# Six more constant products among the transposes of the first head

## The chip, the cores and the metric

The kernel runs on one core of one Trainium2 chip. The metric is device time in microseconds (us) of one execution. A profile shows one execution; its span, from the first to the last instruction, is about 1.7 us shorter than the time (304.4 against 306.14 us before). In these traces TensorE multiplies, VectorE and ScalarE copy, cast and apply functions, GpSimd and SyncE issue most transfers (62 and 92 of 157 in the profile before). All runs told here gave the right result, and those whose state could be judged were fast; a run with a single execution has the state "unknown".

## The reference

```python
# attention over 4 x 8 heads, 768 positions of 64 values, with a mask of 32-blocks
scores = scale * np.matmul(q, k.transpose(0, 1, 3, 2))
...
attn = np.exp(scores); attn = attn / attn.sum(-1, keepdims=True)
x = np.matmul(attn, v)            # heads side by side: (4, 768, 512)
# then a residual MLP
tok = np.einsum('ts,bsd->btd', w_tok, alpha1 * x + beta1)
u = x + lam * tok
out = u + lam * (np.maximum((alpha2 * u + beta2) @ w_ch1, 0) @ w_ch2)
```

## The kernel before

Instructions are placed in a fixed order on each engine by a small planner, which runs when the kernel is built. Ahead of the plan stands a hand-written start for the first head. The parts that matter are these.

```python
def keep_warm(n, w, to=gbT[3]):
    for _ in range(n):          # products of constants; nobody reads the result
        nc.tensor.matmul(to[:, 0:w], ones[:, 0:P], ones[:, 0:w], start=True, stop=True)

keep_warm(6, 512)
keep_warm(1, P)
...                             # VectorE makes the block mask
for w in (0, 1):                # mask product, 24 rows
    nc.tensor.matmul(bq_ps[w][0:NBLK, 0:HS], mbb[MB, :], kx2[0][MB, 0, ts(w, HS)], ...)
...                             # casts of q (VectorE) and k (ScalarE, VectorE)
keep_warm(3, P)
for w, bk, o0, o1, cp in (
    (0, gbT[0], 0, 3, nc.vector.tensor_copy),   # q: three transposes
    (1, gbT[1], 0, 1, nc.scalar.copy),          # k: one
    (1, gbT[2], 1, 3, nc.vector.tensor_copy),   # k: two
):
    t = transposes(bk[:], lambda o: relp[:, 0, w, ts(o, P)], range(o0, o1))
    for r in range(2):
        cp(out=qkr[0][:, w, 0, o0:o1, r, :], in_=t[r * D : (r + 1) * D, o0:o1])
keep_warm(3, P)
...                             # from here on the plan: scores, exponentials, ...
```

The plan's first work is the scores of the first head (five products make two "units" of 1024 columns), seven constant products, the scores of the third unit, six transposes for the second head, one constant product, and the scores of the fourth unit. An exponential on ScalarE follows each unit. On VectorE the plan begins with copies of the mask rows and two casts of q and k for the second head.

The softmax here doesn't subtract the row's maximum and nothing guards it: scores larger than these inputs give would overflow.

## Time and profile before

| | before |
|---|---|
| time, median of three | 306.14 us (305.75 to 306.19) |
| span of the profile | 304.4 us |
| TensorE busy | 99% |
| first product of 128 columns with its full-rate duration (219 ns) starts at | 9.70 us |
| first, fourth, fifth exponential start at | 6.96, 10.44, 11.61 us |

One more view is of use for the comparison: the chain that ended last in order of time, from 4.9 to 9.9 us. The columns are start, duration and what the chain passes through.

```profile
4.89 0.31 ACT relp L541
5.19 0.05 issue
5.24 0.50 PE gb L517 x3
5.74 0.32 PE gb L485 x3
6.06 1.72 PE sps L1019 x5
7.78 0.75 PE gb L485 x7
8.53 0.85 PE sps L1019 x3
9.38 0.54 PE gb L517 x6
```

After the cast of k on ScalarE the chain lies on TensorE alone, through products (L1019 scores, L485 constants, L517 transposes) that still run at half rate (314 ns for 128 columns at 5.5 us, 219 ns from 9.70 us on).

### The profile page before, as it was taken

What the parts mean: (1) busy time and instruction counts of PE and PEld (TensorE: products, weight loads), DVE (VectorE), ACT (ScalarE), POOL (GpSimd) and SP (SyncE); (2) the same over time, 40 slices, a digit from 0 to 9 for tenths busy, and PEclk for the clock granted to TensorE, in tenths of its full rate; (3) what the DMA queues carried; (4) which work ended last, traced back from release to release, by engine and by line L of the source; (5) the groups of instructions that cost most, each with busy time, mean ns of one, the idle gap of its engine ahead of it and who ended that gap; (6) DMA issues with size and microseconds to landing.
All of it is one profiled execution on the core that took longest, in us unless ns stands there. A gap on an engine that the chain in (4) does not pass through costs nothing.

```text
span 304.4 us, 7164 instructions
## 1 busy us (share of the span) xinstructions
PE 300.4 (99%) x2991; PEld 187.9 (62%) x2991; DVE 233.5 (77%) x441; ACT 177.4 (58%) x242; POOL 44.6 (15%) x71
## 2 busy tenths in 40 slices
PE   8999999999999999999999999999999999999996
PEld 3777888766656575566655575555664674665443
DVE  7688899988988995989977886668869681997212
ACT  4999998978778755775486756654657720000000
POOL 9447451150110110020000000000000000000000
DMA  7999999998884959074173423050021004000112
GB/s 157 202 255 209 204 205 180 186 201 138 139 132 91 155 114 164 36 113 93 38 119 45 113 49 74 36 145 4 37 52 43 28 2 122 37 0 0 71 65 73
DMA packets 50672, 31.38 MB, mean 103 GB/s; under 512 B 27784, under 2 KB 47056, under 8 KB 50640
## 3 DMA queue, kind: packets, MB, share of 16 engines
q0 software_dynamic: 17520, 15.47, 32.8%
q1 hardware_dynamic: 32796, 15.06, 21.9%
q8 instruction: 23, 0.38, 0.5%
q10 hardware_dynamic: 324, 0.39, 0.4%
q14 instruction: 9, 0.07, 0.1%
HBM read 30.78 MB, written 6.29 MB: 122 GB/s over the span
## 4 chain that ended last, share of the span: by engine, by line
PE 96%; DVE 2%; ACT 1%; issue 0%; ACTq 0%
PE gb L1529 27%; PE gb L1449 27%; PE gb L1081 12%; PE gb L1302 10%; PE sps L1019 8%; PE sps L1038 4%; PE gb L1038 3%; PE gb L517 2%; PE gb L485 2%; DVE qk L578 1%; ACT eT L1057 0%; ACT qk L576 0%; DVE wtokT L578 0%; DVE ot L1551 0%; DVE x_sb L1100 0%
## 5 line engine op out<-in xcount | busy, mean ns | idle before, releaser
L1057 ACT ACTIVATE eT<-sps 128x1024 f16<-128x1024 f32 x114 | 110.8, 1030 | 9.4 <-PE gb L1081 5.7
L1449 PE MATMUL gb<-uT,w1b 128*128 128x384 bf16 (+1 forms) x512 | 91.8, 326 | 0.0
L1529 PE MATMUL gb<-w2b,hts 128*128 128x512 bf16 (+2 forms) x400 | 89.4, 370 | 0.0
L1449 PEld LDWEIGHTS <-w1b 128*128 128x128 bf16 x512 | 48.6, 98 | 33.7 <-issue 1.9
L1062 DVE TENSOR_TENSOR eT<-eT,msk 128x1024 f16<-128x1024 f16 x90 | 59.6, 683 | 6.5 <-ACT eT L1057 6.4
L1529 PEld LDWEIGHTS <-hts 128*128 128x128 bf16 x400 | 36.7, 98 | 38.9 <-issue 1.9
L1057 ACT ACTIVATE eT<-gb 128x512 f16<-128x512 f32 x60 | 32.5, 594 | 33.8 <-PE gb L1038 31.8
L1496 DVE TENSOR_SCALAR hts<-gb,b1t 128x384 bf16<-128x384 f32 x73 | 44.8, 617 | 9.1 <-PE gb L1449 7.6
L1081 PEld LDWEIGHTS <-eT 128*128 128x128 f16 x1152 | 44.3, 97 | 10.8 <-issue 2.2
L1081 PE MATMUL gb<-vext,eT 128*128 128x65 f16 x1152 | 47.9, 193 | 0.1
L1488 ACT ACTIVATE hts<-gb,b1t 128x384 bf16<-128x384 f32 x55 | 31.5, 581 | 21.4 <-PE gb L1449 19.1
L1302 PE MATMUL gb<-a1p,wtokT 128*128 128x256 bf16 (+1 forms) x360 | 37.0, 251 | 0.0
L1551 DVE TENSOR_TENSOR ot<-x_sb,gb 128x512 f32<-128x512 f32 (+2 forms) x25 | 16.6, 664 | 26.0 <-PE gb L1529 26.0
L1302 PEld LDWEIGHTS <-wtokT 128*128 128x128 bf16 x360 | 29.5, 98 | 6.8 <-issue 1.9
L1019 PE MATMUL sps<-qk 88*128 88x512 bf16 (+1 forms) x144 | 32.6, 336 | 0.2
L1326 DVE TENSOR_TENSOR x_sb<-x_sb,gb 128x512 f32<-128x512 f32 (+1 forms) x26 | 16.7, 641 | 2.9 <-PE gb L1302 2.6
L1100 DVE TENSOR_TENSOR x_sb<-gb,rcp 128x384 f32<-128x384 f32 x32 | 17.8, 557 | 1.1
L1038 PE MATMUL sps<-qk 64*128 64x256 bf16 x180 | 17.9, 305 | 0.0
L1038 PEld LDWEIGHTS <-qk 64*128 64x128 bf16 x240 | 9.3, 94 | 11.5 <-issue 7.1
L1097 DVE RECIPROCAL rcp<-gb 128x6 f32<-128x6 f32 x32 | 6.1, 192 | 13.3 <-PE gb L1081 13.2
L1340 DVE TENSOR_TENSOR ub<-x_sb,a_bc 128x512 bf16<-128x512 f32 (+1 forms) x26 | 16.1, 644 | 0.3
L647 POOL DMA_DIRECT2D v<-in_v_dram x15 | 10.6, 703 | 36.6 <-DVE vext L1119 24.9
(70 smaller groups left out, 173.8 us busy)
## 6 DMA issues: line engine op xcount, KB each, us to landing
out_dram<-ot SPq DMA_DIRECT2D x23, 256.0 KB, 2.0
v<-in_v_dram POOLq DMA_DIRECT2D x16, 192.0 KB, 7.9
k<-in_k_dram POOLq DMA_DIRECT2D x15, 192.0 KB, 7.3
q<-in_q_dram POOLq DMA_DIRECT2D x15, 192.0 KB, 7.5
w1b<-in_moe_w_ch_dram POOLq DMA_DIRECT2D x4, 512.0 KB, 11.8
w2b<-in_moe_w_ch_dram POOLq DMA_DIRECT2D x4, 512.0 KB, 16.9
qk<-qk SPq DMA_DIRECT2D x20, 96.0 KB, 2.3
wtk<-in_moe_w_tok_dram POOLq DMA_DIRECT2D x3, 384.0 KB, 8.2
```

Source lines behind the costliest of these rows:

```text
L1019: nc.tensor.matmul(spsT[sl(key[0])][:, o : o + w], kx2[i][0:KC, a, ts(jt, P)], qx2[i][0:KC, a, c : c + w], start=True, stop=True,)
L1038: nc.tensor.matmul(half(key, r)[:, o : o + w], kd[i][rows, h, g, :], qx2[i][rows, h, c : c + w], start=True, stop=True,)
L1057: nc.scalar.activation(out_, in_, AF.Exp, bias=EXPB, scale=SCALE)
L1062: nc.vector.tensor_tensor(out=e, in0=e, in1=msk[:, :, x : x + 512], op=ALU.mult)
L1081: nc.tensor.matmul(bk[:, t * VW : t * VW + D + 1], eTt[sl(("eT", i))][:, ts(col, P)], vx[:, a, jt, 0 : D + 1], start=(r == 0), stop=(r >= ...
L1100: nc.vector.tensor_tensor(out=x_sb[:, s0 : s0 + NT, h * D : (h + 1) * D], in0=o[:, :, 0:D], in1=rc[:].unsqueeze(2).broadcast_to([P, NT, D] ...
L1302: nc.tensor.matmul(bank(bk)[:, j * wp * P : (j + 1) * wp * P], wtokT[:, s, ts(m * g + j, P)], a1p[sl(ak)][:, s, 0:wp, :].rearrange("p w c ...
L1326: nc.vector.tensor_tensor(out=s, in0=s, in1=tp, op=ALU.add)
L1449: nc.tensor.matmul(bank(bk)[:, 0 : HS + w0], w1b[:, dk, ts(f, P)], rhs[dk], start=(dk == 0), stop=(dk == 3),)
L1488: nc.scalar.activation(htsT[hk][:, f, :], bank(bk)[:, w0 : HS + w0], AF.Relu, bias=b1t[:, f : f + 1], scale=1.0,)
L1496: nc.vector.tensor_scalar(out=htsT[hk][:, f, :], in0=bank(bk)[:, w0 : HS + w0], scalar1=b1t[:, f : f + 1], scalar2=0.0, op0=ALU.add, op1=A ...
L1529: nc.tensor.matmul(bank(ck)[:, cs], htsT[hk][:, nk, ts(mt, P)], w2h["t"][:, nk, cs], start=(nk == 0), stop=(nk == 15),)
```

## The change

The intent is to fill the gaps that TensorE still has before the first scores; the author assumed that its rate then doubles earlier. The whole diff is this.

```diff
     keep_warm(6, 512)
-    keep_warm(1, P)
+    keep_warm(2, P)
...
         t = transposes(bk[:], lambda o: relp[:, 0, w, ts(o, P)], range(o0, o1))
+        keep_warm(1 if w else 4, P)
         for r in range(2):
```

One product is added ahead of the mask product, four between the transposes of q and k, and one after each of the two groups of k. The order of everything else stays.

## The prediction

> **What bounds the kernel now.** I began with the page: the slices of busy tenths, then the chain that ended last.
>
> ```profile
> PE   8999999999999999999999999999999999999996
> ACT  4999998978778755775486756654657720000000
> ...
> PE 96%; DVE 2%; ACT 1%; issue 0%; ACTq 0%
> ```
>
> The reader is to see that TensorE is full in all 40 slices (7.6 us each) and holds 96% of the chain, and that ScalarE is as full only in slices 2 to 6. So work added to TensorE costs time wherever it doesn't land in one of its gaps. The change touches only the first 6 us, so I next read the groups by shape of TensorE, once up to 6.2 us, then from 9.7 to 31 us.
>
> ```profile
> L485 PE MATMUL gb<-const-bfloat16-1.0 128*128 128x128 bf16 x7 | 1.3, 310 | 0.0
> L517 PE MATMUL gb<-identb,relp 128*128 128x128 bf16 x6 | 1.0, 310 | 0.1
> L1019 PE MATMUL sps<-qk 88*128 88x512 bf16 x1 | 0.6, 586 | 0.0
> ```
>
> ```profile
> L1019 PE MATMUL sps<-qk 88*128 88x512 bf16 x29 | 9.9, 379 | 0.1
> L517 PE MATMUL gb<-identb,q 128*128 128x128 bf16 x18 | 2.0, 219 | 0.0
> L485 PE MATMUL gb<-const-bfloat16-1.0 128*128 128x128 bf16 x4 | 0.9, 219 | 0.0
> ```
>
> The same product of 128 columns takes 310 ns early and 219 ns late; the distance from one start to the next goes from 107 ns to 56 ns, and for 512 columns from 427 ns to about 216 ns. TensorE streams at half rate at first. The profile's clock column says 1.00 in all these stretches, so it does not show this; only durations do. One by one, the transposes starting at 9.17, 9.28 and 9.39 us take 314 or 315 ns, those at 9.49, 9.60 and 9.70 take 311, 260 and 219 ns. The step between the starts at 9.599 and 9.696 is 97 ns; 128 columns at 1.2 per ns first and 2.4 after give 87 ns of half rate, so the rate doubled at about 9.68 us.
>
> Third, the timeline of ScalarE, which runs the exponentials:
>
> ```profile
> 5.56 0.55 ACT L552 COPY qk<-gb 64x128 bf16<-64x128 bf16 x2 [0.38 <-PE gb L517]
> 6.96 1.94 ACT L1057 ACTIVATE eT<-sps 128x1024 f16<-128x1024 f32 x2 [0.85 <-PE sps L1019]
> 9.42 13.71 ACT L1057 ACTIVATE eT<-sps 128x1024 f16<-128x1024 f32 x14 [0.52 <-PE sps L1019]
> 23.32 7.61 ACT L1057 ACTIVATE eT<-sps 128x1024 f16<-128x1024 f32 x8 [0.19 <-PE sps L1019]
> ```
>
> It waits for scores at 6.96 and at 9.42 us, and then hardly at all up to 31 us. Whatever brings the first scores forward therefore moves a long row of exponentials with it.
>
> Fourth, the waits in the stretch 4.7 to 5.3 us:
>
> ```profile
> PEld L517 <- ACT relp L541: 0.4, 1, 0.4
> ```
>
> This is the largest real gap of TensorE: products stream until 4.894 us, then the first transpose of k starts at 5.240, after ScalarE's cast (ended 5.184).
>
> [...]
>
> **The change part by part.** It adds six constant products of 128 columns and removes nothing. The order of all other instructions on all engines is unchanged when the two builds are compared. At half rate they cost 6 x 107 = 0.64 us of array time.
>
> 1. One more after the first seven. Stream ended 3.400, next product 3.537: 0.107 us fit in a gap of 0.137. Free.
> 2. Four between the transposes of q and of k: 0.427 us in a gap of 0.346. The first transpose of k goes from 5.240 to about 5.322: 0.08 us late.
> 3. One each after the first and after the last transposes of k. There is no gap there: before, the stream ran on from 5.240 to 5.854, and scores start at 5.914. Now three transposes, two new products and the three old ones end at 5.322 + 8 x 0.1065 = 6.175. The first scores are 0.26 us late.
>
> So taken alone the change costs 0.26 us of TensorE, and about 0.31 us at the first exponential, which must wait for the third product. Its only possible reward is the earlier rate change. [...]
>
> What that gives, followed forward with durations of this trace. First product of scores from 6.175: [...] the two of 256 columns at about 109 ns each start at 6.436 and 6.545; the last, 272 ns long, ends at 6.82, so the first exponential starts near 6.85 (before 6.96). The second follows 0.92 us later as in the trace, 7.77 (7.88). Scores of the third unit wait for the end of the first exponential, 7.88, plus 0.05: 7.93, then 109 + 109 + 377 ns end at 8.53; before, the seven products ahead of them held them to 8.319 and they ended at 9.38. Third exponential near 8.75 instead of 9.42. Here a new wait comes up: the transposes of the second head need VectorE's casts, which ended 8.739 and become some 0.1 us later because of step 2. So they begin near 8.93 (before 9.17), six and one constant product take 7 x 0.056 = 0.39, scores of the fourth unit 0.43 plus 0.16 of drain, fourth exponential 9.96 (10.44). Then 24 products with v, 0.73 us, and the scores of the fifth unit, 0.43: 10.49 + 0.43 + 0.17 = 11.1 against 11.57. Net **0.49 us** gained, with the cost of step 3 already inside. [...]
>
> Does it last? From 11.6 to 31 us ScalarE idles 0.34 us in all and TensorE about 1.5 us, nearly all waiting for exponentials, which move along. After 31 us TensorE has almost no gap. Transfers cannot move, their engines being 90% busy or more up to 76 us; but from the landing records, loads land before first use by 1.2 us (q, 10.22 against 11.41), 0.9 (q, 25.97 against 26.89), 0.8 (v, 33.44 against 34.28) and 0.9 to 1.0 (w2 slices, 58.01 against 58.95, 61.14 against 62.16). All exceed 0.5. So 0.49 us should reach the end: 306.14 - 0.49 = 305.65.
>
> **The rivals.** Rival one: the rate still changes at 9.68 us. [...] Then the lateness of step 3 stays: 306.14 + 0.3 = 306.4. Rival two: the change comes even earlier[...]. Scores then start when VectorE is ready, near 5.9, and the first exponential near 6.6; casts again hold the second head, so some 0.8 us in all, 305.3. [...] Rival three: full rate earlier but all of it swallowed by ScalarE or loads: the slacks above speak against it, time 306.1.
>
> **Range and chances.** I give 0.55 to the change[...] (305.65), 0.15 to earlier still (305.3), 0.25 to no change of the rate (306.4), 0.05 to swallowed. The middle lies at about 305.7; with a run noise of some 0.2 us, 305.0 to 306.5. 2% is 6.1 us[...]: within 2%, 0.98.
>
> **What would show it.** In the profile after, transposes of the second head (near 9 us) should have about 219 ns instead of 314, and scores of 512 columns after 6.3 us 379 instead of 634. The first exponential should start near 6.85, the third near 8.75, the fifth near 11.1. If the first starts near 7.27 and the transposes still take 314 ns, rival one holds. If the constant products at 5 us are already at 219 ns, rival two. If the fifth exponential is 0.5 us early and the span isn't, some wait between 11 and 80 us took it, and the slack argument is wrong.

Terms of the sum place the doubling after the change: the first product of the scores, in which the author took it to fall and which ends at 6.436 us. The sum came to a gain of 0.49 us and 306.14 - 0.49 = 305.65 us; without that assumed moment it doesn't follow. The terms also counted the gaps of TensorE: 0.137 + 0.140 + 0.346 + 0.060 = 0.68 us between 3.40 and 5.91 us in the trace of before, and by the author's estimate 0.030 + 0.140 = 0.17 us after the change. That fewer gaps bring the doubling forward was assumed. The 1.2 and 2.4 columns per ns are 512 columns over the measured 427 and about 216 ns.

## The result, and the profile after

The first comparison gave 305.69 us (305.58 to 305.89, six runs) against 306.14 us (305.75 to 306.59, six runs). The ratio is 0.9985, 95% interval 0.9972 to 0.9998. Ratios here are the mean time of one kernel's fast runs over that of the other's of the same rounds, so they are not quite the ratio of the medians. In later rounds of the same two kernels this gain shrank or vanished; that is told with the experiments. All outputs are right.

The slices and the chain by engine of the changed kernel, from its page:

```profile
PE   8999999999999999999999999999999999999996
ACT  4999999978778755775486756554557720000000
...
PE 91%; DVE 6%; ACT 1%; issue 1%; ACTq 0%
```

TensorE is as full as before, but VectorE has grown from 2% to 6% of the chain. The groups by shape up to 6.2 us, with the mean duration after the busy time:

```profile
L485 PE MATMUL gb<-const-bfloat16-1.0 128*128 128x128 bf16 x14 | 1.8, 250 | 0.0
L517 PE MATMUL gb<-identb,relp 128*128 128x128 bf16 x6 | 0.7, 224 | 0.1
L1020 PE MATMUL sps<-qk 88*128 88x512 bf16 x1 | 0.4, 376 | 0.0
```

The transposes take 224 ns instead of 310, the first scores 376 instead of 586. Here the rate doubled before the transposes: the product starting at 4.46 us took 314 ns, those at 4.57, 4.68 and 4.75 took 287, 237 and 219. ScalarE's timeline:

```profile
5.61 0.55 ACT L553 COPY qk<-gb 64x128 bf16<-64x128 bf16 x2 [0.32 <-PE gb L517]
6.61 2.85 ACT L1058 ACTIVATE eT<-sps 128x1024 f16<-128x1024 f32 x3 [0.45 <-PE sps L1020]
9.84 12.68 ACT L1058 ACTIVATE eT<-sps 128x1024 f16<-128x1024 f32 x13 [0.37 <-PE sps L1020]
22.71 7.61 ACT L1058 ACTIVATE eT<-sps 128x1024 f16<-128x1024 f32 x8 [0.19 <-PE sps L1020]
```

The first exponential is 0.36 us earlier (6.61 against 6.96), the third 0.98 us (8.43 against 9.42), but the fourth only 0.61 us (9.84 against 10.44), and the fifth again 0.61 us (11.00 against 11.61). What came up between is seen in the waits of the stretch 7 to 9.3 us:

```profile
PEld L517 <- DVE relp L512: 0.9, 1, 0.9
...
PE gb L517 <- DVE relp L512: 0.5, 1, 0.5
```

and in the chain in order of time:

```profile
7.73 0.35 DVE qk L997
8.08 0.03 issue
8.11 0.64 DVE relp L512 x2
8.75 0.05 issue
8.80 0.51 PE gb L517 x6
```

TensorE now stands until 8.80 us for VectorE's two casts. These ended at 8.741 us after the change and at 8.739 before, so the transposes of the second head gained only 0.37 us (8.80 against 9.17). The chain goes through VectorE where it had gone through TensorE. Of the 0.61 us at the fifth exponential, 0.49 us are left at 34 us (a copy on ScalarE at 33.92 instead of 34.41), and 0.4 us in the span (304.0 against 304.4). The trace shows what took the difference: one copy on VectorE (L1119 before, L1120 after), on which the work behind it waited. Before, then after:

```profile
32.49 0.35 DVE L1119 COPY vext<-v 128x768 f16<-128x768 f16 x1
```

```profile
31.89 0.53 DVE L1120 COPY vext<-v 128x768 f16<-128x768 f16 x1
```

From 41 us on the exponentials of the two profiles stay 0.43 to 0.44 us apart up to the last one at 239 us. Why the same copy took longer here is not known.

### The profile page after: what moved, and what is told of

Its sections match the earlier page's. It is cut to its first block, busy times and chain, and to the rows that moved or that the text cites. A ratio compares the mean times of both kernels' runs of the same rounds, so it can differ in the third digit from the quotient of the medians.

```text
span 304.0 us, 7157 instructions
## 1 busy us (share of the span) xinstructions
PE 297.9 (98%) x2977; PEld 187.1 (62%) x2998; DVE 234.1 (77%) x441; ACT 177.5 (58%) x242; POOL 44.6 (15%) x71
## 4 chain that ended last, share of the span: by engine, by line
PE 91%; DVE 6%; ACT 1%; issue 1%; ACTq 0%
PE gb L1450 27%; PE gb L1530 27%; PE gb L1082 11%; PE gb L1303 9%; PE sps L1020 5%; PE sps L1039 4%; PE gb L1039 3%; PE gb L517 2%; PE gb L485 1%; DVE qk L579 1%; DVE a1p L1265 1%; DVE a1p L1254 1%; ACT eT L1058 0%; ACT qk L577 0%; DVE x_sb L1101 0%
## 5 line engine op out<-in xcount | busy, mean ns | idle before, releaser
L1530 PE MATMUL gb<-w2b,hts 128*128 128x512 bf16 (+2 forms) x379 | 87.2, 370 | 1.1
L1020 PE MATMUL sps<-qk 88*128 88x512 bf16 (+1 forms) x144 | 31.3, 325 | 0.5 <-ACT eT L1058 0.3
L648 POOL DMA_DIRECT2D q<-in_q_dram x15 | 10.7, 710 | 35.3 <-DMA qk<-q 29.7
```

Of the source, the lines that this page charges most:

```text
L1020: nc.tensor.matmul(spsT[sl(key[0])][:, o : o + w], kx2[i][0:KC, a, ts(jt, P)], qx2[i][0:KC, a, c : c + w], start=True, stop=True,)
L1530: nc.tensor.matmul(bank(ck)[:, cs], htsT[hk][:, nk, ts(mt, P)], w2h["t"][:, nk, cs], start=(nk == 0), stop=(nk == 15),)
```

## The experiments

Two theories stood at the start. **The work decides** (theory 2 in the expectations): the moment of the doubling follows from the products issued, and the gap of 0.35 us at 4.9 us delays it in the kernel before. **Free moment** (theory 1): the moment isn't tied to the kernel, so it differs from run to run, and one profile of each kernel is one draw. All twelve runs were used. The table collects the looks; each row is one profiled execution, with its time at the end. "Full rate" is the start of the first product that has its full-rate duration (219 to 230 ns for 128 columns; 256 columns took 270 to 272 ns at full rate and 421 at half rate in before).

| run | what it is | full rate | exponential 1 / 4 / 5 | time of this execution |
|---|---|---|---|---|
| first profile | before | 9.70 | 6.96 / 10.44 / 11.61 | 306.14 |
| b2 | before again | 4.55 | 6.46 / 9.79 / 10.96 | 305.85 |
| b3 | before again | 4.67 | 6.46 / 10.15 / 11.31 | 306.00 |
| b4 | before again | 5.24 | 6.51 / 9.83 / 11.00 | 305.74 |
| first profile | changed | 4.75 | 6.61 / 9.84 / 11.00 | 305.73 |
| a2 | changed again | 6.15 | 6.85 / 10.06 / 11.22 | 305.95 |
| a3 | changed again | 4.07 | 6.25 / 9.83 / 11.00 | 305.75 |
| a4 | changed again | 5.75 | 6.74 / 9.83 / 11.00 | 305.78 |
| p_first | first product only | 4.14 | 6.32 / 9.84 / 11.00 | 305.80 |
| p_gap | changed, without the four | 4.08 | 6.61 / 9.83 / 11.00 | 305.54 |
| p_four | the four only | 4.99 | 6.54 / 9.82 / 10.99 | 305.77 |
| p_four2 | the four only, again | 5.32 | 6.54 / 9.83 / 11.00 | 305.70 |
| no_warm | no constant products ahead | 10.31 (256 columns) | 7.04 / 10.73 / 11.89 | 306.69 |
| cast_first | changed, casts earlier | 5.85 | 6.73 / 9.46 / 11.08 | 306.13 |

### The kernel before, looked at again (b2, b3, b4)

No edit. Expected:

> The kernel before once more, unchanged, for one look at when the rate of TensorE doubles. Theory 1[...]: the doubling need not be at 9.68 us again[...]. Theory 2 (the moment follows from the work alone: the gap of 0.35 us at 4.9 us delays it): 9.7 us again within 0.2 us. Time 306.1 in either case.

> The kernel before a third time, for one look. By now before has doubled at 9.68 and at 4.46 us, the changed kernel at 4.63 and 6.06. [...] First exponential 6.45 to 6.6 if early, 6.96 if late.

> The kernel before a fourth time, for one look; the same as for b3. If the moment is free, b3, b4 and the two earlier looks shall not all agree.

Measured: the unchanged kernel reached full rate at 4.55, 4.67 and by 5.24 us. In b4 there was no product between 4.89 and 5.24 us, and the one at 4.785 already took only 281 ns. b2's groups from 4.5 to 6.2 us and its ScalarE:

```profile
L517 PE MATMUL gb<-identb,relp 128*128 128x128 bf16 x6 | 0.7, 220 | 0.4 <-ACT relp L541 0.4
```

```profile
6.46 2.86 ACT L1057 ACTIVATE eT<-sps 128x1024 f16<-128x1024 f32 x3 [0.41 <-PE sps L1019]
9.79 4.12 ACT L1057 ACTIVATE eT<-sps 128x1024 f16<-128x1024 f32 x4 [0.47 <-PE sps L1019]
```

This is the profile that the change was meant to bring about, with the 0.4 us gap still in it and without the change. The second theory is right on the point that counts: the moment is not fixed by the kernel. (What moves it is not shown.) b3 adds something else. Its fourth exponential is late (10.15) although its rate doubled early, because a small load (be2T) held VectorE for 0.65 us ahead of the same two casts, which ended near 9.05. So the casts paced this stretch, and their delay cost about 0.3 us at the fourth exponential (9.79 in b2, 9.83 in b4) although the rate had doubled.

### The changed kernel again (a2, a3, a4)

No edit. Expected:

> The changed kernel once more, unchanged. Theory 1: the doubling is at another moment than 4.63 us[...], and the time is 305.5 to 306.0. Theory 2: 4.63 us again within 0.2 us. The time over that of before: 0.9985 as in the first comparison, in either case.

> The changed kernel, to see its spread over runs. So far 28 runs of before lie from 305.48 to 306.63, 13 of them above 306.1; 12 of the changed kernel from 305.55 to 306.07. Theory: before doubles late[...], the changed kernel never does, so the change cuts off the slow part of the spread. Then all six runs here lie under 306.2, before again has about a third above 306.2[...]. Rival: both kernels have the same spread and the twelve were luck; then a third of these runs is above 306.2 too.

> The changed kernel again, as a3: all under 306.2 by the theory, about two of six above 306.2 by the rival. The doubling in the look at a moment other than in the earlier ones.

Measured: full rate from 6.15, 4.07 and 5.75 us, again a different moment each time. The late fourth exponential of a2 (10.06) is not the work of its doubling: as in b3, be2T came late (7.71 us, against 6.47 in the first profile of before), and the casts ended at 8.97. Times: a2 305.71 us median (six runs, 305.55 to 306.07), before 305.88 in the same rounds, ratio 0.9993 [0.9980, 1.0007]. a3 305.69 (five runs, 305.53 to 305.76) and a4 305.79 (five runs, 305.53 to 306.58), before 305.55 (nine runs, 304.98 to 306.54), ratios 1.0000 [0.9987, 1.0012] and 1.0008 [0.9993, 1.0024]. The first comparison's 0.15% did not come back. Putting all rounds together (which were not all run at one time nor on one chip, so this is a rougher comparison than one within rounds), 40 times of before (with the three single ones of b2 to b4) have a mean of 305.90 us, 22 of the changed kernel 305.75 us. The difference is 0.15 us, with a 95% interval of plus or minus 0.16 us worked out from the two spreads, so it isn't clear of zero. Above 306.2 us lie 8 of the 40 and 1 of the 22. That would fit a change that trims the slow part of the spread, but a4's 306.58 contradicts "never", and the counts are too small to show it.

### Parts of the change (p_first, p_four, p_gap, p_four2)

p_first is the kernel before with this edit:

```diff
-    keep_warm(1, P)
+    keep_warm(2, P)
```

> Only the first of the added products (the eighth, ahead of the mask product). Its 0.107 us should show as a later start of the 24-row product (3.64 instead of 3.54 us), since the pause of 0.137 us before that product stays as it is. Theory 2 in the form that the stream up to 4.6 us decides: doubling near 4.63 us as in the changed kernel, and its whole gain, 305.7. Theory 1: the gap at 4.9 us is untouched, so the doubling has the same spread as before; 306.1 to 306.3.

p_four, and p_four2 again, are the kernel before with this one:

```diff
         t = transposes(bk[:], lambda o: relp[:, 0, w, ts(o, P)], range(o0, o1))
+        keep_warm(0 if w else 4, P)
```

> Only the four products between the transposes of q and k. They fill the largest gap. Both theories: if it is this gap that keeps the doubling late, this part has the whole gain, or a little more than the whole change because 0.2 us of other products are absent: 305.5 to 305.7[...]. If the gap doesn't matter: 306.1 to 306.4 and a doubling that is late.

> Only the four products, a second time. The first time gave 305.50 to 306.30, two of six above 306.2. Theory that this gap alone decides: five or six of six under 306.2 and a mean of 305.7, as the changed kernel. If two or more of six are again above 306.2, the four alone do not remove the slow part, and the other two parts of the change, or other causes such as the landing of loads, have a share in it.

p_gap is the changed kernel without its four products:

```diff
-        keep_warm(1 if w else 4, P)
+        keep_warm(1 if w else 0, P)
```

> The changed kernel without its four products between the transposes of q and k, so with the gap at 4.9 us open again and the other two parts kept. Theory: the slow part of the spread is back, one to four of six runs above 306.2, mean 305.9 to 306.2. Rival (the first product or the two late ones matter): all under 306.2.

Measured: p_first 305.76 us, ratio 0.9999 [0.9985, 1.0014]; p_four 305.74, ratio 0.9997 [0.9983, 1.0011]; p_gap 306.21, ratio 1.0016 [1.0001, 1.0031]; p_four2 305.76, ratio 1.0008 [0.9992, 1.0024]. Of p_four's eleven times in the two rounds three lie above 306.2, which is more than the expectation allowed. No part shows a gain. p_gap is a little slower than before in its own rounds, with three of five above 306.2; that agrees in direction with the idea that the open gap brings slow runs, but before has the same gap and had only one of nine above 306.2 in those rounds. So these times don't settle which part matters.

The trace of p_first does settle what the first product costs. TensorE's timeline of before, then of p_first, from 3.2 us:

```profile
3.54 0.49 PE L522 MATMUL sps<-qk,mbb 24*24 24x384 bf16 x1
```

```profile
3.64 0.40 PE L522 MATMUL sps<-qk,mbb 24*24 24x384 bf16 x1
```

The 24-row mask product starts 0.10 us later. In both kernels it starts 0.137 us after the stream of the 128-row product ahead of it ended (3.400 to 3.537; 3.505 to 3.642 in the changed kernel). The pause stayed at 0.137 us with one more product ahead of it; that product did not fill it.

The looks also say something on the gap, though not much. Kernels without the four products were looked at six times (before four times, p_first, p_gap): five reached full rate by 5.24 us and one at 9.70, none in between. Kernels with the four were looked at seven times: five of these reached it between 4.99 and 6.15 us. What makes this pattern no run shows, and thirteen looks are too few to prove one.

### A late doubling on purpose (no_warm)

The kernel before without its constant products ahead of the first scores:

```diff
-    keep_warm(6, 512)
-    keep_warm(1, P)
...
-    keep_warm(3, P)
...
-    keep_warm(3, P)
```

> The kernel before without any of its constant products ahead of the first scores. TensorE then starts at 3.5 us and has gaps up to 5.9 us[...]. This gives the price of a late doubling: first exponential near 6.96, fifth 11.6 or later, and 306.1 to 306.8, that is 0.3 to 0.8 us over runs with an early doubling. If the time is as before (305.9), a late doubling costs nothing in the end.

Measured: 306.96 us median (305.68 to 307.78), ratio 1.0031 [1.0010, 1.0052]; clearly slower, by 0.9 us in the mean. Its groups from 5.9 to 9.9 us and the end of its ScalarE timeline up to 14 us:

```profile
L515 PE MATMUL gb<-identb,relp 128*128 128x128 bf16 x6 | 0.8, 314 | 0.0
```

```profile
10.73 4.02 ACT L1053 ACTIVATE eT<-sps 128x1024 f16<-128x1024 f32 x4 [0.21 <-PE sps L1015]
```

(Line numbers shift with each edit; here L515 is the transpose and L1053 the exponential.) All transposes of the second head still took 314 ns, and full rate came at 10.31 us. The warm-up that the kernel before already has is therefore worth about 0.9 us. In this look the fifth exponential starts 0.89 us later than in most early looks (11.89 against 11.00), behind transposes at half rate: a late doubling is not free. It also shows a spread of 2.1 us, wider than any other kernel's. Only one execution was looked at: that its fast end (305.68) comes from an earlier doubling is a guess, and so is the cause of its slow end.

### The casts earlier (cast_first)

The changed kernel, with VectorE's two casts for the second head put where two copies of mask rows stood; these go where the casts were. The first of the three row copies keeps its place.

```diff
-            lambda op, i=i: first_cast(1, i, nc.vector.tensor_copy),
+            lambda op, i=i: rows[2 + i](op),
...
-        ROWS.append(pl.dve(("row", j), dve(768, 4), (2, 6, 7)[j - 1], e_row))
+        rows[j] = e_row
+        ROWS.append(pl.dve(("row", j), dve(768, 4), (2, 6, 7)[j - 1],
+            e_row if j == 1 else lambda op, j=j: first_cast(1, j - 2, nc.vector.tensor_copy)))
```

(In the kernel that ran, the first line goes through a helper of one line; it does the same.)

> The changed kernel with VectorE's two casts for the second head ahead of two copies of rows that are needed only at 19 us. In the looks with an early doubling TensorE stood from 8.12 to 8.80 us for these casts (their end was 8.74). Theory: with an early doubling this wait is what keeps the gain small; transposes of the second head from about 8.2 us, fourth exponential 9.4 instead of 9.84, fifth 10.4 instead of 11.0, and 0.3 to 0.6 us at the end: 305.1 to 305.4. Rival: loads of the second pair (q lands at 10.2 us) and ScalarE take it up again: 305.7.

Measured: 305.69 us (305.48 to 306.13), ratio 0.9991 [0.9977, 1.0005]; no clear gain. The trace is that of the slowest of its six runs (306.13) and shows what took the gain in that one. ScalarE, then TensorE's two products for the fifth unit, then the waits from 10.4 to 11.3 us:

```profile
6.73 3.77 ACT L1071 ACTIVATE eT<-sps 128x1024 f16<-128x1024 f32 x4 [0.41 <-PE sps L1033]
11.08 3.10 ACT L1071 ACTIVATE eT<-sps 128x1024 f16<-128x1024 f32 x3 [0.58 <-PE sps L1033]
```

```profile
10.22 0.82 PE L1033 MATMUL sps<-qk 88*128 88x512 bf16 x2
```

```profile
PEld L517 <- DMA q<-in_q_dram: 0.8, 1, 0.8
```

The wait for the casts is gone: the transposes start at 8.23 us instead of 8.80, the fourth exponential at 9.46 instead of 9.84. But the fifth exponential starts only at 11.08 (11.00 in the profile after). The load of v landed at 9.06 us here (8.60 there), so VectorE's copy of v and the copies of the second head behind it came late. The latter ended at 10.61, and the second of the two products, which needs them, started at 10.66 instead of following the first at about 10.44. After that the load of q of the second pair, which landed at 11.11, held the next transposes until 11.15 (10.80 in the profile after). In this execution the rival's "loads take it up again" is right; the other five were not looked at. Nothing here beats both kernels clearly.

## Why the prediction was right or wrong

**The time** was predicted as 305.7 us and measured as 305.69. The agreement is luck in part. The case on which it rested, a doubling at the first scores with the first exponential at 6.85, did not occur in the profile after. By the prediction's own sign rival two did: the constant products at 4.98 and 5.04 us took 220 and 221 ns, and the first exponential started at 6.61 (forecast near 6.6). For that case the prediction had 0.8 us and 305.3; it was 0.61 us at the fifth exponential and 0.41 us in the span.

**What bounds the kernel** was read rightly: half rate at first, seen only in durations, and a gap for ScalarE's cast of k. Two readings were loose: the page's DMA digits are 9 only in slices 2 to 9, so the engines are 90% busy from 8 to 68 us, not to 76; and TensorE's first and last slices are 8 and 6.

**Step 1, "Free", was wrong.** The gap of 0.137 us came after the added product as it had come without it. The mask product came 0.105 us later (3.642 against 3.537), and with it the mask's copy on ScalarE (4.490 against 4.384), the cast of k (4.993 against 4.887) and the first transpose of k (5.345 against 5.240). The term for this part should have been 0.105 us of delay, not nothing.

**Steps 2 and 3** were right in kind for an execution that is still at half rate. a4 is one: its first transpose of k started at 5.426 us, which is the predicted 5.322 plus the 0.105 us of step 1. Where the rate has doubled before that, as in the profile after, the four products take 0.22 us (56 to 60 ns from start to start) and fit in the gap.

**The moment of the doubling was the step that failed.** The prediction took the one change seen, at 9.68 us, for that of before, and assumed that the added products would bring it forward to the first scores. It was another in each of the eight executions of the two kernels that were looked at. The unchanged kernel doubled near 4.5 us two times, and by 5.24 us a third time, in three further looks. Rival two had allowed for another moment in each run, but the sum used the one profile as if it were typical, so the base from which 0.49 us was to be gained was a slow draw. The bare difference between before and after is 0.45 us in the first rounds, 0.15 plus or minus 0.16 us over all of them.

**The forward sum was right in its mechanism.** It named the casts as the new wait: fourth exponential predicted 9.96, measured 9.84; fifth about 11.1, measured 11.00. The casts were not made 0.1 us later, as it had assumed (they ended at 8.74 before and after), and the fifth exponential of before had started at 11.61; the sum's 11.57 is the end of its scores in the chain. The repeats make this stronger. Nine looks of before, the changed kernel and its parts reached full rate between 4.07 and 5.75 us without a held-up cast; their first exponentials spread from 6.25 to 6.74 us, and their fourth ones all started between 9.79 and 9.84. Up to there a doubling at 5.75 us was worth as much as one at 4.07; the casts ended at 8.74 us before and after.

**"Does it last?" mis-sized one slack and left out two loads and VectorE.** The q of the second pair was given 1.2 us, from one landing at 10.22 us. In the other looks at before, the changed kernel and its parts it landed from 10.08 to 11.02 us, in cast_first at 11.11. In the profile after, a weight load waited 0.2 us for it, but the products in front streamed on until the transposes started at 10.80, so it cost nothing there; in p_first (landing 11.02) the transposes started at 11.07, and of 0.61 us at the fifth exponential 0.37 were left at the seventh. Not in the list at all were be2T and v, which held VectorE (be2T in b3 and a2, v in cast_first), and VectorE's copies of v, which took about 0.35 us in most looks and 0.5 us or more in some, as in the profile after.

**Rival one** (no change of the rate) did not occur in any look at the changed kernel. **What stays open:** how often before doubles late (one look of four), whether its times above 306.2 us are those executions (none of them was profiled), and what sets the moment. A rival for the slow times is untested: late loads and slow copies on VectorE. In each look the lead of the exponentials over the first profile of before is fixed from 41 us on, and it gives the time of that execution within 0.06 us. With an early doubling this lead was 0.31, 0.19 and 0.45 us for before (b2, b3, b4) and 0.43, 0.21, 0.39 and 0.40 us for the changed kernel (after, a2, a3, a4). What spreads these is not the doubling, and the two ranges overlap.

## What to carry to other kernels

A single profile of each kernel can show a difference that lies between two executions, not between two kernels: before explaining a few tenths of a microsecond at the start of a kernel, profile the unchanged one again. Before filling a gap, ask whether it is waiting time and what paces the work just behind it: here the pause of 0.137 us stayed, VectorE's casts (until 8.74 us) took up part of what an earlier full rate could give, and in some executions a load or a copy took up more (be2T held VectorE for 0.65 us in b3). Read the rate of TensorE from durations of one shape: in before the clock column said 1.00 from 0 to 13 us, while 128 columns took 314 ns up to 9.4 us and 219 from 9.70 on.
